# Leaving the state update out of the last chunk of a chunked linear attention

## The chip, the cores and the metric

The kernel runs on one core of a Trainium2 chip. The metric is the device time of one execution in microseconds (us). Before the change three runs gave 1142.96, 1143.62 and 1143.84 us, a median of 1143.62 us.

## The reference

The reference has three parts, one after the other, all in 32-bit floats. The first is a gated linear attention over 768 positions, for 4 batches, 8 heads and a head width of 48, with a complex decay `a` per position and channel:

```
mag = sqrt(a_re^2 + a_im^2);  a = a * min(mag, 0.999) / (mag + 1e-6)
for t in range(768):
    S = a[t] * S + k[t] (outer) v[t]        # S complex, k and v real
    y[t] = q[t] . Re(S)
```

Its output, seen as 3072 tokens of width 384, goes through `relu(x @ w_in)^2 @ w_out` (inner width 2048) and then through `(silu(x @ w_gate) * (x @ w_val)) @ w_out` (inner width 1536). The state S is not an output: only y of each position is.

## The kernel before

**Chunks.** The 768 positions are cut into six chunks of 128. Within a chunk the attention is written with matrices: with running products P of the decay, the keys are divided by P (tile `ks`) and the queries multiplied by it (tile `qs`); the masked product of the two, times v, is what the chunk's own positions give, and `qs` times the state that the chunk before left is the rest. The state that a chunk hands on is (its old state + scaled keys times v), scaled by the decay of the whole chunk.

**elem** (lines 493 to 649) makes these factors for one chunk. It computes the decay products, the chunk's total decay (`last`, `lm`), from that the scale `yB` (lines 596 to 601 and 632) and the new `phase` (line 630), and per group of two heads the tiles `qs` and `ks`. The keys are needed by position for the state, so `ks` is written to DRAM (`scr`, line 646) and read back in another layout as `kn` (line 647).

**mat** (lines 652 to 736) does the matrix part for one group of two heads; a chunk has four groups, called groups 0 to 3 here. TensorE transposes `ks` and `qs` into PSUM (`pt`), ScalarE copies them out (`kT`, `qT`). Lines 680 to 687 bring the scale of the state into the state's layout: a copy `ysrc` on ScalarE, two small products `pr`, a reciprocal `rho` on VectorE. Then come the scores `sc`, the masking `pb` on VectorE, the output `py` (from state and from scores), and its copy `ys`, which DMAs put into `xf`, the input of the next part (lines 713 to 725). Lines 726 to 735 are the state's update: eight products `pu` of `kn` and `vt`, and on VectorE two operations of 96x384, one that adds `pu` to the state and one that multiplies it by `rho`.

**moe1 and moe2** (lines 868 and 923) are the two other parts, chunk by chunk. Each float product is made of three products of 32-bit operands that are split into a high and a low half (`xh`, `xl`, `gh`, `gl`). One step of moe1 is nine matmuls into a tile `h`, ScalarE's relu, square and cast (`u`, `u`, `gh`), VectorE's `gl`, and two steps later nine matmuls into the accumulators `acc`. moe2 has two tiles per step, `pg` and `pv`, and a silu.

**prep2** (line 834) converts the 36 weight tiles of moe2: a load `wst`, three integer operations `wt` on VectorE, a cast into `wc` or `wr` on ScalarE, a subtraction on VectorE, and two operations on ScalarE that check `wst` (with their accumulators). A converted tile needs a free place. The first nine places are the attention's own tiles, when the last chunk has done with them (line 1040): `qs`, `ks`, `kn`, `cm`, `X` and four parts of `an`. The others are places of moe1's weights, as the last chunk of moe1 frees them.

**What sets the order.** `fast` (line 1024) pairs the attention of chunk n+1 with moe1 of chunk n; the last attention (chunk 5) goes beside moe1 of chunk 4, then moe1 of chunk 5 beside prep2, then moe2. All operations are recorded with a rank and a cost, and a list scheduler (`arrange`, line 172) puts them in the order in which each engine will issue them; it starts an operation as soon as its engine, its inputs and its buffers are free by its costs, the lowest rank first. Each engine then works through its list in that order. An edit in one place thus moves instructions around it.

Of the kernel before, what the change touches and what calls it, by code (L numbers as in the profile page):

```python
# [9 lines left out]
F32 = mybir.dt.float32  # L10
F32R = mybir.dt.float32r
I32 = mybir.dt.int32
AF = mybir.ActivationFunctionType
# [295 lines left out]
class Kern:  # L309
# [183 lines left out]
    def elem(self, n, g0, NG, res):  # L493

        nc, G, D, W = self.nc, self.G, self.D, self.W
        t0, nb = self.chunks[n]
        VW = NG * W
        gs = range(g0, g0 + NG)
        smn = lambda nm: self.e2.tile([128, nb, W], F32, name=nm, tag="smn", bufs=self.NSMN)
        sml = lambda nm: self.e2.tile([128, nb, W], F32, name=nm, tag="smk", bufs=self.NSMK)  # L500
        cs = lambda nm, shape: self.e2.tile(shape, F32, name=nm, tag=f"cs{len(shape)}", bufs=6 - len(shape))
# [3 lines left out]
        cols = lambda i, k=1: slice(i * W, (i + k) * W)  # L505
# [7 lines left out]
        def out(name, shape, i):  # L513
            if n:
                return self.e2.tile(shape, F32, name=name, tag=name, bufs=1)
            return self.slot(name, shape, F32, i)
# [5 lines left out]
        for i in gs:  # L522
# [17 lines left out]
            r = b0  # L540
# [19 lines left out]
        ks0 = slice(g0 * W // 32, g0 * W // 32 + K)  # L560
# [32 lines left out]
        sq2 = cs("sq2", [128, 2, K])  # L593
        nc.scalar.activation(out=sq2, in_=last, func=AF.Square)
        yield
        yB = self.e2.tile([128, VW], F32, name="yB", tag="yB", bufs=1)

        nc.vector.tensor_tensor(out=lm, in0=sq2[:, 0], in1=sq2[:, 1], op=ALU.add)
        nc.scalar.activation(out=sq2[:, 0], in_=lm, func=AF.Ln, bias=self.tiny[:, 1:2])
        yt = self.ytile[:, ks0]  # L600
        nc.scalar.activation(out=yt[:, :, 0], in_=sq2[:, 0], func=AF.Exp, scale=-0.5)
        for i in gs:
            if i % 2 == 0:

                for r in range(2):
                    self.cmul(an[:, :, r, cols(i, 2)], an[:, :, r, cols(i, 2)], an[:, :, 3, cols(i, 2)], 2 * W)
                    yield
                self.cmul(an[:, :, 2, cols(i, 2)], an[:, :, 1, cols(i, 2)], an[:, :, 2, cols(i, 2)], 2 * W)
                yield
                for c in range(2):  # L610
                    nc.vector.transpose(out=an[:, c, 3, cols(i, 2)], in_=X0[:, 32 * K * c + (i - g0) * W + 1:][:, 0:2 * W])
                yield
            pp = an[:, :, :, cols(i)]
            kq = keys.pop(i, None) or self.load(n, i, (self.k, self.q))
            kt, qt = kq[:, 0], kq[:, 1]
            psq = self.e2.tile([128, 2, nb, W], F32, name="Bt", tag="pp", bufs=self.NPP)
            nc.scalar.activation(out=psq, in_=pp, func=AF.Square)

            qs = out("qs", [128, nb, G, 2, D], 12 + i)
            for c in range(2):  # L620
                nc.vector.tensor_tensor(out=qs[:, :, :, c], in0=v4(pp[:, c]), in1=perm(qt), op=ALU.mult)
            yield
            pm = xy = sml("pm")
            nc.vector.tensor_tensor(out=pm, in0=psq[:, 0], in1=psq[:, 1], op=ALU.add)
            lp = sml("lp")
            nc.scalar.activation(out=lp, in_=pm, func=AF.Ln, bias=self.tiny[:, 1:2])
            iv = lp
            nc.scalar.activation(out=iv, in_=lp, func=AF.Exp, scale=-1.0)
            if i == g0:
                nc.vector.tensor_tensor(out=self.phase[:, :, ks0], in0=last,  # L630
                                        in1=yt[:, :, 0].unsqueeze(1).to_broadcast([128, 2, K]), op=ALU.mult)
                nc.vector.transpose(out=yB, in_=yt.rearrange("p k i -> p (k i)"))
            yield
            nc.vector.tensor_tensor(out=xy, in0=pm, in1=iv, op=ALU.mult)
            niv = xy
            nc.vector.scalar_tensor_tensor(out=niv, in0=xy, scalar=2.0, in1=iv, op0=ALU.subtract, op1=ALU.mult)
            yield
            ki = xy
            nc.vector.tensor_tensor(out=v4(ki), in0=perm(kt), in1=v4(niv), op=ALU.mult)
            ks = out("ks", [128, nb, G, 2, D], 16 + 2 * i)  # L640
            for c in range(2):
                nc.vector.tensor_tensor(out=ks[:, :, :, c], in0=v4(pp[:, c]), in1=v4(ki), op=ALU.mult)
            L = 32 * nb
            scr = self.dr.tile([self.B, L, G * 2 * D], F32, name="scr", tag="scr")
            kn = out("kn", [L, self.B, G, 2 * D], 17 + 2 * i)
            nc.sync.dma_start(out=scr.rearrange("b (j r) x -> (b j) (r x)", r=nb), in_=ks.rearrange("p r h c d -> p (r h c d)"))
            nc.sync.dma_start(out=kn.rearrange("p b h x -> p b (h x)"), in_=scr.rearrange("b t x -> t b x"))
            res[i] = dict(qs=qs, ks=ks, kn=kn, yB=yB[:, cols(i - g0)], vt=self.load_v(n, i))
            yield


    def mat(self, n, g, r, xf):
# [18 lines left out]
        for h in range(G):  # L671
            for src, dst, nm in ((ks, kT, "kT"), (qs, qT, "qT")):
# [4 lines left out]
                                        src[:, rr, h].rearrange("p c d -> p (c d)"), self.ident)  # L677
                nc.scalar.copy(dst[h], pt)
                yield
        rho = self.e2.tile([2 * D, G, B], F32, name="rho", tag="rho", bufs=self.N_rho)  # L680
        pr = bank("pr", [2 * D, G, B])
        ysrc = self.e2.tile([128, G, 2, D], F32, name="ysrc", tag="ysrc", bufs=self.N_ysrc)
        nc.scalar.copy(ysrc, yB.rearrange("p (h d) -> p h d", h=G).unsqueeze(2).to_broadcast([128, G, 2, D]))
        for h in range(G):
            nc.tensor.matmul(pr[:, h], ysrc[:, h].rearrange("p c d -> p (c d)"),
                             self.ident.rearrange("p (b j) -> p b j", b=B)[:, :, 0], start=True, stop=True)
        nc.vector.reciprocal(out=rho, in_=pr)
        yield
        pbs = []
        for h in range(G):  # L690
            sc = bank("sc", [L, B, L])
            for b in range(B):
                nc.tensor.matmul(sc[:, b], kT[h][:, L * b:L * b + L], qT[h][:, L * b:L * b + L], start=True, stop=True)
            pb = self.e2.tile([L, B, L], F32, name="pb", tag="pb", bufs=self.N_pb)
            nc.vector.tensor_tensor(
                out=pb, in0=sc,
                in1=self.mask[0:L, 0:L].unsqueeze(1).to_broadcast([L, B, L]), op=ALU.mult)
            pbs.append(pb)
            yield

            if h % 2 == 1:
                py = bank("py", [128, B, L])
                for b in range(B):
                    if n:
                        for hh in (h - 1, h):
                            o = 64 * (hh % 2)
                            nc.tensor.matmul(py[o:o + D, b], self.state[:, h0 + hh, b],
                                             qT[hh][:, L * b:L * b + L], start=True, stop=False)
                    for hh in (h - 1, h):
                        o = 64 * (hh % 2)  # L710
                        nc.tensor.matmul(py[o:o + D, b], vt[:, b, hh], pbs[hh][:, b], start=n == 0, stop=True)
                yield
                ys = self.e2.tile([128, B, L], F32, name="ys", tag="ys", bufs=self.N_ys)
                for hh in range(2):
                    o = 64 * hh
                    nc.scalar.activation(out=ys[o:o + D], in_=py[o:o + D], func=AF.Copy, scale=-1.0,
                                         accum_out=self.yflag[o:o + D, (n * self.H + h0 + h) // 2:][:, 0:1])
                    hd = (h0 + h - 1 + hh) * D
                    d0 = 0
                    while d0 < D:  # L720
                        row = hd + d0
                        m = min(D - d0, 128 - row % 128)
                        nc.sync.dma_start(out=xf[row % 128:row % 128 + m, row // 128],
                                          in_=ys[o + d0:o + d0 + m].rearrange("p b l -> p (b l)"))
                        d0 += m
                pu = bank("pu", [2 * D, 2, B, D])
                hs = h - 1
                for hh in range(2):
                    for b in range(B):
                        nc.tensor.matmul(pu[:, hh, b], kn[:, b, hs + hh], vt[:, b, hs + hh], start=True, stop=True)  # L730
                st = self.state[:, h0 + hs:h0 + hs + 2]
                if n:
                    nc.vector.tensor_tensor(out=st, in0=pu, in1=st, op=ALU.add)
                nc.vector.tensor_tensor(out=st, in0=st if n else pu,
                                        in1=rho[:, hs:hs + 2].unsqueeze(3).to_broadcast([2 * D, 2, B, D]), op=ALU.mult)
                yield
# [475 lines left out]
```

## Time and profile before

| | |
|---|---|
| median of three runs | 1143.62 us |
| the profiled execution | 1144.72 us, of which the span of instructions is 1142.6 us |
| TensorE (PE) busy | 1067.2 us, 93% of the span |
| VectorE (DVE) busy | 705.8 us, 62% |
| ScalarE (ACT) busy | 619.3 us, 54% |

A view of the profile gives starts in us from the beginning of the span. "PEld" is the load of a matmul's stationary operand. Nearly every line of the trace reads L306, the line that issues what was recorded, so groups are told apart by tile names. The attention of the last chunk runs its matrix part from 540 to 601 us, moe1 of chunk 5 begins at 614 us and moe2 at 685 us.

### The profile page before, as it was taken

The numbers are of one execution on the slowest core, as the hardware profiler recorded it, in microseconds if no ns is written. First come the engines' busy times: TensorE is split into PE (matmuls) and PEld (weight loads), VectorE is DVE, ScalarE is ACT, GpSimd is POOL, SyncE is SP. The second block draws the span as 40 slices with busy tenths as digits, with TensorE's granted clock in tenths as the row PEclk, the third lists the DMA queues.
The fourth block names the chain that finished last, engine by engine and source line by source line (L and its number), as shares of the span: only waits on it lengthen the run. The fifth ranks groups of instructions, "written<-read, shape, count | busy, mean of one in ns | idle before, by whom it ended". The sixth has DMA issues, their size and how long they took to land.

```text
span 1142.6 us, 16426 instructions
## 1 busy us (share of the span) xinstructions
PE 1067.2 (93%) x5890; PEld 899.9 (79%) x5890; DVE 705.8 (62%) x1485; ACT 619.3 (54%) x1334; POOL 1.0 (0%) x7
## 2 busy tenths in 40 slices
PE   2458979999999999999999999999999999999997
PEld 0346857888888888888887878888888888888886
DVE  6998999799789789789658883232232222322221
ACT  6479879957766766866669993131221222211221
POOL 0000000000000000000000000000000000000000
PEclk9968989999999999999999999999999999999998
DMA  5345355403612621522536441010010100000000
GB/s 141 125 128 160 111 150 164 131 15 92 160 55 71 164 72 56 154 56 69 153 99 211 148 124 56 1 56 1 1 56 1 56 1 1 28 1 1 28 1 31
DMA packets 102490, 89.25 MB, mean 78 GB/s; under 512 B 35072, under 2 KB 90368, under 8 KB 102400
## 3 DMA queue, kind: packets, MB, share of 16 engines
q1 hardware_dynamic: 102080, 87.93, 26.6%
q8 instruction: 48, 0.79, 0.3%
q14 instruction: 42, 0.34, 0.1%
q10 hardware_dynamic: 320, 0.20, 0.1%
HBM read 64.49 MB, written 18.87 MB: 73 GB/s over the span
## 4 chain that ended last, share of the span: by engine, by line
PE 79%; ACT 9%; DVE 6%; DMA 2%; SPq 2%; issue 1%; ACTq 0%; DVEq 0%
PE acc L306 26%; PE h L306 13%; PE pg L306 13%; PE pv L306 13%; PE py L306 4%; ACT wst L306 3%; PE pt L306 3%; PE sc L306 3%; PE pu L306 3%; SPq L306 2%; ACT u L306 2%; DVE an L306 1%; DMA wst<-in_moe_w_in_dram 1%; DVE AB L306 1%; ACT gh L306 1%
## 5 line engine op out<-in xcount | busy, mean ns | idle before, releaser
L306 ACT CAST gh<-u 128x512 fp32r<-128x512 f32 x168 | 104.2, 621 | 247.3 <-PE acc L306 217.0
L306 PE MATMUL h<-xh,wc 128*128 128x512 f32 x576 | 199.2, 400 | 3.2 <-ACT xh L306 2.4
L306 PE MATMUL acc<-gh,wr 128*128 128x512 f32 x576 | 195.7, 396 | 0.1
L306 DVE TENSOR_TENSOR gl<-u,gh 128x512 fp32r<-128x512 f32 x168 | 115.3, 688 | 126.6 <-ACT gh L306 125.9
L306 DVE TENSOR_TENSOR u<-pv,u 128x512 f32<-128x512 f32 x72 | 49.8, 692 | 204.6 <-PE pv L306 203.4
L306 PE MATMUL acc<-wr,gh 128*128 128x384 f32 x576 | 146.8, 335 | 0.0
L306 PE MATMUL pg<-xh,wc 128*128 128x512 f32 x396 | 134.8, 394 | 1.1 <-ACT xh L306 1.1
L306 PE MATMUL pv<-xh,wc 128*128 128x512 f32 x396 | 133.8, 392 | 1.3 <-ACT u L306 1.3
L306 PEld LDWEIGHTS h<-xh,wc 128*128 128x128 f32 x576 | 108.8, 190 | 27.7 <-ACT xh L306 2.7
L306 PEld LDWEIGHTS acc<-gh,wr 128*128 128x128 f32 x576 | 108.0, 188 | 23.3 <-issue 1.7
L306 PE MATMUL h<-xl,wc 128*128 128x512 f32 x288 | 114.4, 397 | 0.7 <-DVE xl L306 0.7
L306 PE MATMUL acc<-gl,wr 128*128 128x512 f32 x288 | 113.7, 395 | 0.2 <-DVE gl L306 0.2
L306 PEld LDWEIGHTS acc<-wr,gh 128*128 128x128 f32 x576 | 105.1, 188 | 5.2
L306 ACT ACTIVATE u<-pg 128x512 f32<-128x512 f32 x72 | 43.1, 599 | 104.7 <-PE pg L306 104.7
L306 PE MATMUL acc<-wr,gl 128*128 128x384 f32 x288 | 96.6, 335 | 0.0
L306 PEld LDWEIGHTS pv<-xh,wc 128*128 128x128 f32 x396 | 74.3, 188 | 18.3 <-ACT u L306 1.7
L306 PEld LDWEIGHTS pg<-xh,wc 128*128 128x128 f32 x396 | 74.3, 188 | 16.2 <-ACT xh L306 1.5
L306 ACT ACTIVATE u<-h 128x512 f32<-128x512 f32 x96 | 57.1, 597 | 46.1 <-PE h L306 41.0
L306 PE MATMUL pg<-xl,wc 128*128 128x512 f32 x198 | 78.2, 395 | 0.1
L306 PE MATMUL pv<-xl,wc 128*128 128x512 f32 x198 | 77.8, 393 | 0.0
L306 DVE SCALAR_TENSOR_TENSOR wt<-wst,wt 128x384 int32<-128x384 int32 x136 | 74.0, 551 | 1.7
L306 DVE TENSOR_TENSOR AB<-an 128x768 f32<-128x768 f32 x72 | 68.3, 948 | 0.6
(132 smaller groups left out, 1751.3 us busy)
## 6 DMA issues: line engine op xcount, KB each, us to landing
wst<-in_moe_w_out_dram SPq DMA_DIRECT2D x28, 384.0 KB, 3.5
scr<-ks SPq DMA_DIRECT2D x24, 384.0 KB, 2.5
kn<-scr SPq DMA_DIRECT2D x24, 384.0 KB, 3.5
wst<-in_moe_w_in_dram SPq DMA_DIRECT2D x16, 384.0 KB, 3.6
in<-in_k_dram SPq DMA_DIRECT2D x96, 48.0 KB, 2.0
in<-in_q_dram SPq DMA_DIRECT2D x96, 48.0 KB, 2.0
vt<-in_v_dram SPq DMA_DIRECT2D x48, 96.0 KB, 2.9
x2d<-x SPq DMA_DIRECT2D x18, 256.0 KB, 2.1
```

What stands on the lines that cost most here:

```text
L306: o.call(*o.args, **o.kw)
```

## The change

For the last chunk (`final`) elem no longer makes `yB` and the new `phase`, writes no `scr` and reads no `kn`; mat no longer makes `ysrc`, `pr` and `rho`, and leaves out `pu` and the two operations on the state. The output of the last chunk is computed as before. The tile of the tag `kn`, the third of the nine places of prep2, is then last used by chunk 4.

```diff
+        final = n == len(self.chunks) - 1
...
-        yB = self.e2.tile([128, VW], F32, name="yB", tag="yB", bufs=1)
-
         nc.vector.tensor_tensor(out=lm, in0=sq2[:, 0], in1=sq2[:, 1], op=ALU.add)
-        nc.scalar.activation(out=sq2[:, 0], in_=lm, func=AF.Ln, bias=self.tiny[:, 1:2])
-        yt = self.ytile[:, ks0]
-        nc.scalar.activation(out=yt[:, :, 0], in_=sq2[:, 0], func=AF.Exp, scale=-0.5)
+        if not final:
+            yB = self.e2.tile([128, VW], F32, name="yB", tag="yB", bufs=1)
+            nc.scalar.activation(out=sq2[:, 0], in_=lm, func=AF.Ln, bias=self.tiny[:, 1:2])
+            yt = self.ytile[:, ks0]
+            nc.scalar.activation(out=yt[:, :, 0], in_=sq2[:, 0], func=AF.Exp, scale=-0.5)
...
-            if i == g0:
+            if i == g0 and not final:
...
+            kn = None
+            if not final:
+                scr = self.dr.tile([self.B, L, G * 2 * D], F32, name="scr", tag="scr")
+                kn = out("kn", [L, self.B, G, 2 * D], 17 + 2 * i)
+                nc.sync.dma_start(out=scr.rearrange("b (j r) x -> (b j) (r x)", r=nb), in_=ks.rearrange("p r h c d -> p (r h c d)"))
+                nc.sync.dma_start(out=kn.rearrange("p b h x -> p b (h x)"), in_=scr.rearrange("b t x -> t b x"))
+            res[i] = dict(qs=qs, ks=ks, kn=kn, yB=None if final else yB[:, cols(i - g0)], vt=self.load_v(n, i))
...
+        if kn is not None:
+            rho = self.e2.tile([2 * D, G, B], F32, name="rho", tag="rho", bufs=self.N_rho)
...
+            nc.vector.reciprocal(out=rho, in_=pr)
+            yield
...
+                if kn is None:
+                    yield
+                    continue
                 pu = bank("pu", [2 * D, 2, B, D])
```

The scheduler's order moves with it. In the rows below a number behind a tile's name only tells tiles of one name apart.

TensorE, the last group of the last attention, before (`h_1534` is a step of moe1 of chunk 4, `acc_1335` an accumulator of the same):

```order
L306 MATMUL pt<-ident,qs 96x128 x4
L306 MATMUL pr<-ident,ysrc 96x4 x2
L306 MATMUL sc<-qT,kT 128x128 x4
L306 MATMUL h_1534<-xh,wc 128x512
...
L306 MATMUL sc<-qT,kT 128x128 x4
L306 MATMUL py<-qT,state 48x128 x2
L306 MATMUL py<-pb,vt 48x128
L306 MATMUL pu<-vt,kn 96x48 x4
L306 MATMUL py<-pb,vt 48x128
...
L306 MATMUL pu<-vt,kn 96x48 x4
L306 MATMUL acc_1335<-gh,wr 128x512
```

and now (`h_1514` is the next step of moe1):

```order
L306 MATMUL pt<-ident,qs 96x128 x4
L306 MATMUL sc<-qT,kT 128x128 x4
L306 MATMUL acc_1335<-gh,wr 128x512
L306 MATMUL acc_1335<-gl,wr 128x512
L306 MATMUL sc<-qT,kT 128x128 x4
...
L306 MATMUL py<-qT,state 48x128 x2
L306 MATMUL py<-pb,vt 48x128 x2
...
L306 MATMUL h_1514<-xh,wc 128x512
```

The `pr` and `pu` are gone, the two score products stand two matmuls apart instead of nine, and three steps of moe1 of chunk 4 follow the last `py` instead of two.

ScalarE, where moe1 of chunk 4 ends, before (`xh<-xf` splits the input of moe1 of chunk 5, `xh<-x_1648` that of moe2's first chunk, and `h_1547` is the last step of moe1 of chunk 4):

```order
L306 ACTIVATE u<-h_1547 128x512
L306 ACTIVATE wst,flg_60<-wst,wlow_98 128x384
L306 ACTIVATE u<-u 128x512
L306 CAST xh<-xf 128x512
L306 CAST gh<-u 128x512
L306 CAST xh<-xf 128x512 x2
...
L306 COPY x_1554<-acc_1337 128x512
...
L306 CAST wc<-wt 128x384
L306 CAST xh<-x_1648 128x512 x2
```

and now (`h_1522` is that last step, `x_1623` moe2's first input):

```order
L306 CAST xh<-xf 128x512 x2
L306 ACTIVATE u<-h_1522 128x512
L306 CAST xh<-xf 128x512
L306 ACTIVATE u<-u 128x512
...
L306 CAST gh<-u 128x512
...
L306 COPY x_1529<-acc_1337 128x512
L306 CAST xh<-x_1623 128x512 x2
```

The split of `xf` has moved ahead of the last step's relu, and the split of moe2's input follows the copies at once.

TensorE, where moe1 of chunk 5 ends and moe2 begins, before (`acc_1587` is moe1's last accumulator):

```order
L306 MATMUL acc_1587<-gh,wr 128x512
L306 MATMUL pv<-xh,wc 128x512 x2
...
L306 MATMUL pv<-xh,wc 128x512
L306 MATMUL pg<-xl,wc 128x512
...
L306 MATMUL pg<-xh,wc 128x512
L306 MATMUL pv<-xh,wc 128x512
L306 MATMUL pv<-xl,wc 128x512
```

and now (`acc_1562` is that accumulator):

```order
L306 MATMUL acc_1562<-gh,wr 128x512
L306 MATMUL pv<-xh,wc 128x512
L306 MATMUL pg<-xh,wc 128x512
L306 MATMUL pg<-xl,wc 128x512
...
L306 MATMUL pg<-xh,wc 128x512
L306 MATMUL pv<-xh,wc 128x512
L306 MATMUL pv<-xl,wc 128x512
```

Before, fifteen matmuls (seven `pv`, eight `pg`) stood between the last `acc` and moe2's second `pv`; now ten do (one and nine), since more of the first pair has moved ahead of moe1's steps.

## Rows read from the trace of the kernel before

**Rows 1.** The page, part 1: busy us, share of the span, instructions

```profile
PE 1067.2 (93%) x5890; PEld 899.9 (79%) x5890; DVE 705.8 (62%) x1485; ACT 619.3 (54%) x1334; POOL 1.0 (0%) x7
```

**Rows 2.** Stretch, length, busy us (instructions) of PE, PEld, DVE, ACT, POOL; PEclk; DMA

```profile
540.00:560.00 20.00, 20.00 (x144) 17.07 (x143) 14.55 (x31) 14.89 (x30) 0.00 (x0) 1.00 0.44 135
560.00:580.00 20.00, 20.00 (x149) 17.08 (x148) 10.34 (x23) 10.89 (x24) 0.00 (x0) 1.00 0.52 144
...
610.00:620.00 10.00, 8.87 (x39) 6.68 (x38) 7.25 (x15) 9.52 (x26) 0.00 (x0) 1.00 0.68 218
...
640.00:660.00 20.00, 20.00 (x90) 16.55 (x89) 18.43 (x38) 20.00 (x55) 0.00 (x0) 1.00 0.53 159
...
680.00:700.00 20.00, 18.38 (x81) 14.51 (x80) 10.25 (x19) 13.19 (x29) 0.00 (x0) 1.00 0.24 79
```

**Rows 3.** The chain that ended last, 545 to 565 us: start, us, what

```profile
545.72 0.26 PE pr L306 x4
...
549.08 2.04 PE h L306 x9
...
558.24 1.32 PE pu L306 x16
559.55 0.88 PE pt L306 x8
...
563.65 2.19 PE h L306 x9
```

**Rows 4.** A group over all six chunks: count, busy us, mean ns, idle before

```profile
L306 ACT COPY ysrc<-yB 128x192 f32<-128x192 f32 x24 | 8.4, 350 | 4.7 <-DVE yB L306 4.7
```

**Rows 5.** TensorE's instructions from 607 to 627 us: start, us, what, idle before

```profile
607.84 0.39 PE L306 MATMUL h<-xh,wc 128*128 128x512 f32 x1
...
614.51 0.39 PE L306 MATMUL h<-xh,wc 128*128 128x512 f32 x1
...
618.37 0.39 PE L306 MATMUL h<-xh,wc 128*128 128x512 f32 x1
619.88 0.50 PE L306 MATMUL pg<-xh,wc 128*128 128x512 f32 x1 [1.12 <-ACT xh L306]
...
627.30 0.40 PE L306 MATMUL h<-xh,wc 128*128 128x512 f32 x1
```

**Rows 6.** The way of moe2's first input; last, landing times around there

```profile
613.96 0.34 SPq L306 DMA_DIRECT2D x<-x2d  x1
...
619.21 1.13 ACT L306 CAST xh<-x 128x512 fp32r<-128x512 f32 x2
...
DMA to landing us min/median/max: 4.8/4.9/6.6
```

**Rows 7.** ScalarE and TensorE where moe2 begins

```profile
685.08 1.11 ACT L306 COPY x<-acc 128x512 f32<-128x512 f32 x2
686.04 0.71 ACT L306 ACTIVATE wst<-wst,wlow 128x384 f32<-128x384 f32 x1
...
688.37 1.28 ACT L306 ACT_TABLE_LOAD   x1
689.66 0.60 ACT L306 ACTIVATE u<-pg 128x512 f32<-128x512 f32 x1
...
688.62 0.40 PE L306 MATMUL pg<-xh,wc 128*128 128x512 f32 x1
690.31 0.50 PE L306 MATMUL pv<-xh,wc 128*128 128x512 f32 x1 [1.30 <-ACT u L306]
```

**Rows 8.** ScalarE's first conversion of prep2; the DMA queue's issues around it

```profile
590.66 0.52 ACT L306 CAST wc<-wt 128x384 fp32r<-128x384 f32 x1
...
558.31 0.38 SPq L306 DMA_DIRECT2D wst<-in_moe_w_out_dram  x1
...
586.40 1.79 SPq L306 DMA_DIRECT2D xf<-ys  x3
597.70 0.37 SPq L306 DMA_DIRECT2D wst<-in_moe_w_val_dram  x1
```

More of the change, by code (lines that the diff above doesn't have):

```diff
@@ L643, in elem @@
             L = 32 * nb
[L644 to L648, printed above, removed]
+            kn = None
[5 more added lines that the diff above has]
+            res[i] = dict(qs=qs, ks=ks, kn=kn, yB=None if final else yB[:, cols(i - g0)], vt=self.load_v(n, i))
             yield
@@ L679, in mat @@
                 yield
[L680 to L688, printed above, removed]
+        if kn is not None:
+            rho = self.e2.tile([2 * D, G, B], F32, name="rho", tag="rho", bufs=self.N_rho)
+            pr = bank("pr", [2 * D, G, B])
+            ysrc = self.e2.tile([128, G, 2, D], F32, name="ysrc", tag="ysrc", bufs=self.N_ysrc)
+            nc.scalar.copy(ysrc, yB.rearrange("p (h d) -> p h d", h=G).unsqueeze(2).to_broadcast([128, G, 2, D]))
+            for h in range(G):
+                nc.tensor.matmul(pr[:, h], ysrc[:, h].rearrange("p c d -> p (c d)"),
+                                 self.ident.rearrange("p (b j) -> p b j", b=B)[:, :, 0], start=True, stop=True)
+            nc.vector.reciprocal(out=rho, in_=pr)
+            yield
         pbs = []
```

## The prediction, made before the result was known

> **What bounds the kernel now.** I read the busy times first. TensorE is busy for 93% of the span, VectorE for 62, ScalarE for 54 [rows 1]. A busy share is an average, so I took the stages that the change touches. From 540 to 580 us, the matrix part of the last attention beside moe1 of chunk 4, TensorE is busy without a gap at a granted clock of 1.00 (the 2.4 GHz level), VectorE for 14.55 and then 10.34 of 20 us, ScalarE for 14.89 and then 10.89 of 20 [rows 2]. The reader is to see that the other engines have room there and TensorE has none. Next comes the chain that ended last: through that stretch it runs from one TensorE group to the next, and `pr` and `pu` stand in it [rows 3]. So what these take there is on the path.
>
> Two later places matter, since TensorE gets there sooner after the change. At 610 to 620 and at 680 to 700 us it is not full: 8.87 of 10 and 18.38 of 20 [rows 2]. The instructions name the waits: at 618.6 us for ScalarE's `xh` [rows 5], at 688.9 us for ScalarE's silu, which follows its table load [rows 7]. And from 640 to 660 us ScalarE is busy for 20.00 of 20 us beside TensorE's 20.00 [rows 2]: there two engines are near the limit together, which makes the main doubt below.
>
> **The change part by part.** *The products.* In the chain the sixteen matmul instructions of a group's `pu` (eight products, each in two passes) take 1.32 us, and the four of `pr` 0.26 us [rows 3]. The chunk has four groups: 4 x 1.32 = 5.28 us and 4 x 0.26 = 1.04 us, together 6.32 us. I take all of it as gain, because TensorE neither waits nor idles in that stretch: what stands behind these products is moe1, which is ready. The bound from below is that the last group's share, 1.58 us, is lost in waits for `kT`, `qT` or `pb`, since the scores now stand closer together; that leaves 4.7.
>
> *The turns between kinds of matmul.* Nine matmuls of moe1 take 2.04 us behind scores and 2.19 us behind `pr` [rows 3]: a turn costs up to 0.15 us. The new order has 32 turns where there were 36, counted from the steps before the last attention's matrix part to moe2. Two of the four are entries into moe1's matmuls, 2 x 0.15 = 0.3 us of gain; the range is 0 to 0.6.
>
> *ScalarE, VectorE and the DMA queue.* Four copies `ysrc` of 350 ns [rows 4] leave ScalarE, eight operations on the state and four reciprocals leave VectorE, and eight DMAs leave the queue. Beside a full TensorE I price all that at nothing; if the cover were gone, ScalarE's 4 x 0.35 = 1.4 us would be the gain. No wait is added.
>
> *What the freed place does.* The first conversion of prep2 starts at 590.66 us [rows 8], when the attention's last transposes let go of its tiles; the weights behind it then share the few buffers of `wt`. Now the third weight finds `kn` free, and in ScalarE's new list its cast stands ahead of the last group's copies `kT` and `qT`. So conversions start earlier, in a stretch where ScalarE had 9.1 of 20 us to spare [rows 2]. That is why I expect it to keep pace with a TensorE that is 6.6 us further on.
>
> *The gap at 619 us.* From the first step of moe1 of chunk 5 at 614.51 to its fourth at 627.30 us TensorE issues 48 matmuls (three steps of nine `h`, and 21 of `pg`, `pv` and `acc`) [rows 5]. At 2.04/9 = 0.227 us each they need 10.88 us; 12.79 passed, so 1.9 us are lost. The cause is a row of steps: moe2's input is loaded into the buffer of `xf`, so the load waits for the split of `xf`; it was issued at 613.96 us, and its own split began at 619.21 [rows 6]. The load lands 4.8 to 6.6 us after its issue [rows 6]. In the new order the split of `xf` stands ahead of the last relu of moe1 of chunk 4, and the attention ends one step of moe1 earlier. The last `h` of that step was issued by 607.84 + 0.23 = 608.07 us [rows 5], so the old load came 5.9 us behind it. With two casts ahead of the relu, only the relu, one cast and its subtraction on VectorE are left: two ScalarE operations in a row take 1.13 us [rows 6], and with as much again for the subtraction and the hand-overs I get some 2.7 us. The load then lands 7.5 to 9.3 us behind that step. TensorE has 27 + 18 matmuls to issue before it needs it, 45 x 0.227 = 10.2 us, and the first two casts of its split take 1.13 us [rows 6], the subtraction some 0.7. So most of the gap goes: I take 1.6 us of gain, with bounds 0 and 1.9.
>
> *The gap at 689 us.* TensorE's last `pg` of 688.62 us ends its issue at 688.85 and the next `pv` starts at 690.31 [rows 7]: 1.46 us, because all three PSUM buffers wait for silu, which waits for ScalarE's copies of the accumulators (from 685.08), two splits and a table load of 1.28 us. The new order has ten matmuls in front of that wait where there were fifteen, so TensorE comes to it 5 x 0.227 = 1.1 us earlier; ScalarE's list has one check of `wst` less between the copies and the table load, some 0.6 us by its row of 0.71 [rows 7]. I take 1.1 - 0.6 = 0.5 us of loss, with bounds from 1.4 of gain (ScalarE gets there with nothing left to do) to 2.0 of loss (it is as late as before and the cover is gone).
>
> *The sum.* 6.32 + 0.3 + 1.6 - 0.5 = 7.7 us. The profiled execution took 1144.72 us, its span 1142.6; less 7.7 that is 1137.0. The three runs have a median of 1143.62, 1.1 us below the profiled one, so I predict 1135.9 us. The bounds together: at best 6.32 + 0.6 + 1.9 + 1.4 = 10.2 us, at worst 4.7 + 0 + 0 - 2.0 = 2.7 us.
>
> *A rule to weigh.* The price of `pu` stands on its spacing, 1.32 / 16 = 82 ns, though it moves only 48 columns; a transpose `pt`, with 128 columns, has 0.88 / 8 = 110 ns [rows 3]. The Trainium skill, "TensorE: Matmul & The Clock Gate", section "Back-to-back issue gap", puts a matmul of 1 to 64 columns at about 25 ns. By that rule the sixteen would be worth 0.4 us and a group's `pr` 0.1, and the first term 2.0 us instead of 6.32. Its section on LDWEIGHTS gives columns / 1.2, 80 ns for 96 columns, an estimate that the 82 ns agree with: the load of `kn` is what the removed products pay for. I go by the row.
>
> **The rivals.** *ScalarE holds the gain back (in part or whole).* From 640 us on ScalarE is as full as TensorE [rows 2]. If its conversions do not start earlier, moe1 of chunk 5 soon waits for its relu and casts, and the end moves only by what ScalarE itself is spared: 1.4 us of `ysrc`. In full that gives 1143.6 - 1.4 = 1142.2 us; halfway, 1139.0. For it speaks the 20.00 of 20; against it that ScalarE has idle time before 600 us, and that the slots of prep2 are freed by moe1's own progress, so its work is paced by TensorE.
>
> *The products are cheaper than their spacing.* If only the columns counted, sixteen `pu` would take 16 x 48/128 x 0.110 = 0.66 us, `pr` next to nothing, and the first term were 2.7 us: 1143.6 - (2.7 + 0.3 + 1.6 - 0.5) = 1139.5 us. Against it: in the chain the transposes start when the last `pu` is done, and 1.32 us are seen to pass [rows 3]. This is the side on which the page's 25 ns stand.
>
> *Slower: a cast blocks ScalarE's line.* ScalarE works in order. The third weight's cast now stands ahead of the last group's `kT`; that weight's load stands in the DMA queue behind `ys` of an earlier group. The queue has paused for long in this stretch: between the end of one issue at 588.2 and the next at 597.70 us lie 9.5 us [rows 8]. If such a pause falls on this load, ScalarE stands at the cast, TensorE has no transposed keys, and with moe1's step ahead used up it waits up to 9.5 us in the last group, and what leans on `xf` waits too. The change is slower than before from a wait of 7.7 us on; with 9.5 us and the gap at 619 us kept (1.6) it comes to 1143.6 - 7.7 + 9.5 + 1.6 = 1147.0 us. Against it: it is the third of prep2's loads, which in the old trace was issued at 558.31 us, 32 us before the first cast [rows 8].
>
> *Nothing is gained.* If moe1 of chunk 5 begins when `xf` lands and not when TensorE is done, the time stays at 1143.6. Against it: the new order has one step of moe1 more between the last `py` and the end of moe1 of chunk 4, 18 x 0.227 = 4.1 us in which `xf` can land.
>
> **How the numbers follow.** The forecast, all terms about as above (1134.3 to 1138.0 us): 0.68. ScalarE holds back: 0.15, of which 0.12 still ends below 1141.3. Cheaper products: 0.03. More than forecast, below 1134.3, because the gap at 689 us closes as well: 0.06. Nothing gained: 0.03. Slower: 0.05. A difference of 0.2% (2.3 us) is about what a measurement of this kernel can tell from no change. Faster by more than that: 0.68 + 0.12 + 0.03 + 0.06 = 0.89; within it 0.03 + 0.03 = 0.06; slower 0.05. The range of 8 in 10 leaves out the slow cases and the fullest form of the first rival, and has room for the best case of the bounds: 1133.8 to 1140.3 us.
>
> **What would show it.** In the changed profile the chain through the last attention must still be TensorE's, without `pu` and `pr`, and moe1 of chunk 5 must begin some 6.6 us earlier, near 608 us; `xh` must no longer stop `pg`; the gap before moe2's second `pv` must be about 2 us; the first cast of prep2 must come ahead of 585 us. I am wrong if TensorE idles in the last group behind ScalarE's `kT` or `qT`, if moe1 of chunk 5 runs at more than 2.04 us per nine matmuls, or if its first step starts earlier by much less than the removed time.

## The result and the profile after

| | before | after |
|---|---|---|
| median | 1143.73 us (4 runs, 1142.96 to 1144.24) | 1133.31 us (4 runs, 1132.51 to 1133.58) |
| ratio, 95% interval | | 0.9906 [0.9893, 0.9918] |
| profiled execution, its span | 1144.72, 1142.6 us | 1133.17, 1131.1 us |

The change is worth 10.4 us here, and 12.0 in a second set (below). The forecast was 7.7 us, and the time lies 0.5 us below its range.

The page's busy times, which answer to [rows 1], lose 11.6 us on TensorE, 4.3 on VectorE and 2.1 on ScalarE:

```profile
PE 1055.6 (93%) x5810; PEld 891.0 (79%) x5810; DVE 701.5 (62%) x1471; ACT 617.2 (55%) x1328; POOL 0.9 (0%) x7
```

The windows that answer to [rows 2] (start and end, length, then the busy time of PE, PEld, DVE, ACT and POOL, the granted clock, DMA share and GB/s):

```profile
540.00:560.00 20.00, 20.00 (x135) 16.94 (x133) 14.35 (x30) 14.87 (x30) 0.00 (x0) 1.00 0.32 88
560.00:580.00 20.00, 20.00 (x165) 17.15 (x163) 11.29 (x22) 13.57 (x31) 0.00 (x0) 1.00 0.37 106
640.00:660.00 20.00, 20.00 (x90) 16.54 (x89) 18.47 (x39) 20.00 (x57) 0.00 (x0) 1.00 0.53 156
660.00:680.00 20.00, 17.79 (x76) 13.79 (x74) 14.67 (x30) 19.90 (x50) 0.00 (x0) 1.00 0.28 90
```

TensorE is as full as before in the last attention. From 660 to 680 us, where moe1 now gives way to moe2, it has holes (17.79 of 20), as it had from 680 to 700 us before [rows 2], while ScalarE is busy for 19.90. The chain through two groups of the last attention (start, duration, engine and tile), which answers to [rows 3]:

```profile
560.36 0.89 PE sc L306 x8
561.25 0.24 PE h L306
561.49 0.89 PE sc L306 x8
562.38 1.84 PE h L306 x8
564.23 1.90 PE py L306 x32
566.12 0.57 PE pt L306 x4
...
572.16 1.79 PE sc L306 x16
573.95 0.57 PE py L306 x6
574.51 0.89 PE acc L306 x3
575.41 1.67 PE py L306 x26
```

It is still all TensorE, without `pr` and `pu`. Look also at `py`: in the first of these groups its 32 instructions stand in one row. In the same view of the kernel before, the group that follows [rows 3] has its `py` cut twice by a single matmul of moe1:

```profile
567.63 0.36 PE py L306 x4
567.98 0.43 PE acc L306
568.41 0.35 PE py L306 x2
568.76 0.42 PE acc L306
569.19 1.67 PE py L306 x26
```

The last attention has five such rows of `py` now, where it had eight. That is the first thing the prediction did not see.

The prediction read the chain up to 565 us. Further on, the same view of the kernel before leaves TensorE at 588 us:

```profile
585.89 2.17 PE h L306 x9
588.07 0.02 issue
588.09 0.60 ACT u L306
```

From there it runs mostly through ScalarE, up to moe2's second `pv` at 690 us. In the changed kernel it stays with TensorE up to 601 us, and from 616 to 680 us it is mostly ScalarE's. ScalarE thus had little to spare before the change as well. The gain passes here with ScalarE's work starting earlier too (its first cast of prep2 below); no run holds that work alone back.

TensorE's instructions that answer to [rows 5] and [rows 7] (an idle time before one, and what ended it, in brackets), and ScalarE's that answer to [rows 6] and [rows 8]:

```profile
605.42 0.39 PE L306 MATMUL h<-xh,wc 128*128 128x512 f32 x1
609.29 0.39 PE L306 MATMUL h<-xh,wc 128*128 128x512 f32 x1
609.52 0.40 PE L306 MATMUL pg<-xh,wc 128*128 128x512 f32 x1
...
672.44 0.39 PE L306 MATMUL acc<-gh,wr 128*128 128x512 f32 x1
673.50 0.50 PE L306 MATMUL acc<-gh,wr 128*128 128x512 f32 x1 [0.67 <-ACT gh L306]
674.22 0.50 PE L306 MATMUL acc<-gl,wr 128*128 128x512 f32 x1 [0.22 <-DVE gl L306]
...
678.28 0.40 PE L306 MATMUL pg<-xh,wc 128*128 128x512 f32 x1
680.04 0.50 PE L306 MATMUL pv<-xh,wc 128*128 128x512 f32 x1 [1.36 <-ACT u L306]
```

```profile
574.28 0.51 ACT L306 CAST wr<-wt 128x384 fp32r<-128x384 f32 x1 [0.82 <-DVE wt L306]
...
606.11 1.15 ACT L306 CAST xh<-x 128x512 fp32r<-128x512 f32 x2
```

moe1 of chunk 5 begins at 605.42, not 614.51 us. Its first `pg` follows `h` with no wait: `xh` is cast 3.4 us ahead of it. The first cast of prep2 comes at 574.28, not 590.66 us. The wait for silu is 0.06 us longer than before. The waits for `gh` and `gl` ahead of it stood there before the change too, 0.57 us shorter:

```profile
682.18 0.98 PE L306 MATMUL acc<-gh,wr 128*128 128x512 f32 x2
683.38 0.50 PE L306 MATMUL acc<-gl,wr 128*128 128x512 f32 x1 [0.22 <-DVE gl L306]
```

Last, what lies behind TensorE's last product `tot`, which starts at 1134.27 us before and at 1123.99 after. The view is that of the program's last line, ten waits of SyncE with their first and last start; first the kernel before, then after:

```profile
L1207 SPq EVENT_SEMAPHORE  x10: 17/28/28, 1140.0 to 1142.6; - x10
```

```profile
L1215 SPq EVENT_SEMAPHORE  x10: 17/28/28, 1129.8 to 1131.0; - x10
```

The same ten waits took 2.6 us and take 1.2. In the kernel before, SyncE pauses 1.29 us among them; afterwards it does not.

**The account.** The cost of a TensorE instruction is counted here as the distance from its start to the next start, summed by tile. The anchors are the first `pt` of chunk 4 (449.92 us before, 448.71 after), the first `h` of moe1 of chunk 5, the second `pv` of moe2, and `tot`.

| stretch | before | after | gain | of which |
|---|---|---|---|---|
| start to chunk 4's first `pt` | 449.92 | 448.71 | 1.21 | differs between executions (below) |
| to moe1 of chunk 5 | 164.59 | 156.71 | 7.88 | `pu` 5.66, `pr` 1.13, `py` 0.89, `sc` 0.37, the rest -0.17 |
| to moe2's second `pv` | 75.80 | 74.61 | 1.19 | gap at 619 us 1.80, waits for `gh`, `gl` and silu -0.64, the rest 0.03 |
| to `tot` | 443.96 | 443.95 | 0.0 | |
| to the end of the span | 8.35 | 7.07 | 1.28 | SyncE's pause |

Without the first line this is 10.35 us, and the medians differ by 10.42. In all the traces of this study the first `pt` of chunk 4 lies between 448.1 and 451.5 us, so the first line is not counted as the change's.

### The profile page after: what moved, and what is told of

It reads as the page before. It is cut to its first block, busy times and chain, and to the rows that moved or that the text cites. A ratio compares the mean times of both kernels' runs of the same rounds, so it can differ in the third digit from the quotient of the medians.

```text
span 1131.1 us, 16229 instructions
## 1 busy us (share of the span) xinstructions
PE 1055.6 (93%) x5810; PEld 891.0 (79%) x5810; DVE 701.5 (62%) x1471; ACT 617.2 (55%) x1328; POOL 0.9 (0%) x7
## 4 chain that ended last, share of the span: by engine, by line
PE 78%; ACT 9%; DVE 7%; DMA 2%; SPq 2%; issue 2%; ACTq 0%; DVEq 0%
PE acc L306 25%; PE pg L306 13%; PE pv L306 13%; PE h L306 13%; PE py L306 4%; PE pt L306 3%; PE sc L306 3%; ACT wst L306 3%; PE pu L306 2%; SPq L306 2%; DVE AB L306 2%; ACT u L306 1%; DVE an L306 1%; ACT gh L306 1%; DVE wt L306 1%
```

## The experiments

The kernel before ran along in each set: median 1144.41 us beside the first four, 1144.33 beside the next four, 1144.76 beside the last three. Ratios are to that.

**The scale alone put back** into the changed kernel (`yB`, `ysrc`, `pr`, `rho`).

```diff
-        if kn is not None:
+        if True:
```

> The changed kernel, with the scale of the last chunk put back alone: yB, ysrc, pr, rho, without pu and without the state. By the count of TensorE's starts in the two traces pr is worth 1.13 us, and since the order cuts the py of a group as often as before (8 rows of py instead of 5) 3 cuts at some 0.33 us come on top: the last attention takes 2.1 us longer than in the changed kernel, the gap at 619 us stays closed, the time is about 1135.4 us. By the forecast's sizes (1.04 for pr, 0.3 for turns) 1.3 us, 1134.6 us.

Measured: 1138.42 us, 0.9952 [0.9939, 0.9966]. From chunk 4's first `pt` to moe1 of chunk 5 it takes 159.88 us, 3.17 more than the changed kernel: `pr` 1.14, `py` 1.08 (eight rows again; 0.26 of it lies in chunk 4, where nothing was edited), `sc` 0.37, `acc` 0.51. So `pr` costs some two and a half times its own time, because with it the order tears `py` as before. The other way round, `pu` and the state alone are worth 164.59 - 159.88 = 4.71 us, less than their own 5.66. The gap at 619 us stays closed. The whole loss, 5.1 us between the medians, is larger than the 2.1 expected: in the profiled execution one fall of the clock (last section) cost another 1.56 us.

**The place of `kn` held**: round trip put back, and one column of `kn` read at each group's end, no products.

```diff
-            kn = None
-            if not final:
...
+            res[i] = dict(qs=qs, ks=ks, kn=None if final else kn, held=kn,
...
+                    nc.vector.tensor_copy(self.ytile[:, 0, 1:2], r["held"][:, 0, 0, 0:1])
```

> The changed kernel, with the key round trip (scr, kn) of the last chunk put back, and a read of one column of kn at the end of each group, so that kn's place is free for prep2 as late as before; no products. If the freed place closed the gap at 619 us (the split of xf stands behind the last relu again), the gap comes back with up to 1.8 us; if the gap closed because the attention ends earlier, it stays closed. The attention stage itself as in the changed kernel (within 0.2 us). SyncE's list is as long as before: if its length makes the pause of 1.3 us among its last waits, that comes back too: 1136.4 us with both, 1133.3 with neither.

Measured: 1135.48 us, 0.9919 [0.9905, 0.9932]; the pause of SyncE is back (8.31 us behind `tot`). The gap is back too:

```profile
609.90 0.39 PE L306 MATMUL h<-xh,wc 128*128 128x512 f32 x1
611.41 0.50 PE L306 MATMUL pg<-xh,wc 128*128 128x512 f32 x1 [1.12 <-ACT xh L306]
```

So the freed place did close the gap, by way of ScalarE's order: here the split of `xf` stands behind the last relu of moe1 of chunk 4 again. But the waits at 673 and 680 us shrink by 1.3 us in return, the stretch to moe1 of chunk 5 takes 0.47 us less (I had allowed 0.2), and from chunk 4's first `pt` to `tot` this kernel takes 675.25 us, the changed one 675.27. The freed place is worth nothing in the end. Nor do the conversions need it to start earlier: with the place held, the first cast of prep2 comes at 581.81 us, still 8.9 us ahead of the kernel before.

**`py` held together, in the last chunk of the kernel before.** The scheduler lets `py` start only when both masks are done, puts it ahead of all else, and `pu` behind it.

```diff
+                if n == len(self.chunks) - 1:
+                    for o in nc.ops[k0:k1]:
+                        o.after.update(masked)
+                        o.rank -= 10 ** 6
```

> The kernel before, all its work, but in the last chunk the scheduler holds the py of a group together (4 rows of py instead of 8, pu behind the last py). By the count a cut costs some 0.33 us: 1.3 us less in the last attention, whose products are all there. The split of xf now stands ahead of the last relu, so the gap at 619 us closes as well if the order makes it: together 3.1 us, 1140.6 us; without the gap 1142.4. If a turn costs 0.15 us as the forecast had it and most turns stay, 0.6 us or nothing.

Measured: 1142.27 us, 0.9976 [0.9967, 0.9985]. With four rows of `py` instead of eight, and all products in place, `py` costs 1.30 us less from chunk 4 on (1.17 of it in the last chunk), `sc` 0.52, `pu` 0.41: 2.23 us. The other tiles take 0.24 more, so the stretch is 1.99 us shorter, 0.50 for each row that goes. That is more than I expected. By the forecast's count nothing should have been gained: between moe1's matmuls and the attention's there are 42 turns in this order where there were 36. The gap near 619 us did not close, it broke up into smaller waits (1.75 us together). There my expectation rested on a misreading: in this order too the split of `xf` stands behind the last relu of moe1, as in the kernel before. So this run does not speak against the cause.

**The state update of chunk 4 left out as well.**

```diff
+        nostate = n >= len(self.chunks) - 2
...
-            if not final:
+            if not nostate:
```

> The changed kernel, with the state update of chunk 4 left out as well (its output for the last chunk then lacks what chunk 4 hands on). By the count chunk 4's attention gets shorter by pr 1.13, pu 5.65 and 3 cuts of py of some 0.33, 7.8 us, with no gap of prep2 in it: 1125.5 us. By the forecast's sizes 6.6 us, 1126.7 us. If much of the last chunk's gain came from the places it frees and not from TensorE's time, less than 5 us.

Measured: 1127.74 us, 0.9856 [0.9842, 0.9869]. From chunk 4's first `pt` to moe1 of chunk 5: 149.86 us, 6.85 less than the changed kernel. My 7.8 was wrong in one point: chunk 4 keeps its eight rows of `py`. The products' 6.78 us are left, and they are TensorE's own time. The medians differ by 5.6 us only, since 0.78 us is lost again behind `tot`, where SyncE pauses at another point (last section).

**`py` held together in chunks 1 to 5** of the changed kernel (the edit above for all `n` but 0).

> The changed kernel, with the py of a group held together by the scheduler in chunks 1 to 5 (4 rows of py in a chunk instead of 10, 11, 11, 8 and 5). If each cut costs what the run with uncut py in the last chunk showed (2.23 us for 4 rows, over py, sc and pu), the 25 rows that go are worth 9 to 12 us, less what the wait for both masks costs: 1122 to 1126 us. If cuts are cheap (0.15 us a turn) some 4 us, 1129 us. If py now waits for VectorE's masks, nothing or a loss.

Measured: 1129.21 us, 0.9872 [0.9854, 0.9890]: some 4 us below the changed kernel, not 9 to 12. That is the size that I had put beside cheap cuts. Yet `py` costs 7.6 us in each chunk where it took up to 9.5, 7.1 us less over the five chunks. So the rows are not cheap, but what they cost in the last chunk cannot be multiplied by their number. In chunks 4 and 5 only 0.3 us is left of it: their stretch is 6.4 us shorter, but 27 matmuls of moe1 (6.1 us at 0.227) now stand ahead of it. Part is lost again: in chunk 4 the transposes `pt`, with waits in them, take 8.35 us instead of 6.67, and the waits for `gh`, `gl` and silu, at 668 and 673 us there, grow by 0.8 us.

**ScalarE's second check left out** for moe2's weights.

```diff
+            if self.used[2] <= 2 * self.F1 // 128:
                 nc.scalar.activation(out=hi, in_=hi, func=AF.Relu, scale=-1.0, bias=self.wlow2, accum_out=f2)
```

> The changed kernel without the second of ScalarE's two checks on each weight of moe2 (36 operations of some 0.7 us, 25 us of ScalarE between 575 and 750 us; that part of the check of the inputs is left out). If ScalarE is what TensorE waits for at 673 and 680 us (3.1 us in the changed kernel), most of the wait at 673 us and part of that at 680 us go: 1.5 to 3 us less, 1130.3 to 1131.8 us. If these waits come from the chain acc, copies, table load, silu alone, under 0.5 us.

Measured: 1129.29 us, 0.9866 [0.9851, 0.9882]. The stretch from moe1 of chunk 5 to moe2's second `pv` takes 71.89 us instead of 74.61, and no wait is left at either place. ScalarE's backlog, with the checks in it, made both, also the one that I had put down to the copies, the table load and silu. The median is 4.0 us below the changed kernel, more than my 1.5 to 3: 2.7 us come from this stretch, 0.6 from the one ahead of it, and the rest is not explained.

**SyncE's list made as long as before**: eight small loads in the last chunk's elem of the changed kernel.

```diff
+            for j in range(8):
+                nc.sync.dma_start(out=self.ytile[0:32, 0, 1 + j:2 + j], in_=self.v[0, 0, 0:32, j:j + 1])
```

> The changed kernel with eight small loads (32 numbers each, read by nobody) in SyncE's list during the last chunk's elem, so that the list is as long again as before the change. If its length sets the pause of 1.3 us among SyncE's last waits, the span after TensorE's last product is 8.3 us again instead of 7.1 and the time 1134.6 us, with TensorE as in the changed kernel. If the pause comes from anything else the change left out, 1133.3 us.

Measured: 1135.66 us, 0.9922 [0.9908, 0.9936]. TensorE's stretches are those of the changed kernel (156.57, 74.60 and 443.94 us, `tot` at 1124.73), and the pause is back. The time is 1.1 us above the 1134.6 that I gave; in the profiled execution chunk 4 is reached 0.9 us later.

```profile
L1218 SPq EVENT_SEMAPHORE  x10: 17/28/28, 1130.5 to 1132.9; - x10
```

**`pu` with half of `kn` as its stationary operand**, in the last chunk of the kernel before.

```diff
+                        half = D if n == len(self.chunks) - 1 else 2 * D
-                        nc.tensor.matmul(pu[:, hh, b], kn[:, b, hs + hh], vt[:, b, hs + hh], start=True, stop=True)
+                        nc.tensor.matmul(pu[0:half, hh, b], kn[:, b, hs + hh, 0:half], vt[:, b, hs + hh], start=True, stop=True)
```

> The kernel before, but in the last chunk pu takes 48 of kn's 96 columns as its stationary operand (half of the state, which nobody reads after that chunk); as many products, as many columns moved. If the load of the stationary operand sets the 82 to 88 ns, the 64 products cost about half: 2.8 us less in the last attention, 1141 us. If a product of 48 columns has a floor of its own, its 88 ns stay and the time is that of the kernel before.

Measured: 1140.99 us, 0.9967 [0.9955, 0.9979]. The instructions of `pu` in the last attention (nanoseconds, smallest, median and largest; first and last start; the stationary operand's size), in the kernel before and here:

```profile
L306 PEld LDWEIGHTS pu<-vt,kn x64: 159/165/165, 557.8 to 599.7; 128*96 128x96 f32 x64
L306 PE MATMUL pu<-vt,kn x64: 205/248/283, 558.1 to 599.7; 128*96 128x48 f32 x64
```

```profile
L306 PEld LDWEIGHTS pu<-vt,kn x64: 119/125/125, 559.6 to 597.3; 128*48 128x48 f32 x64
L306 PE MATMUL pu<-vt,kn x64: 204/208/243, 559.6 to 597.3; 128*48 128x48 f32 x64
```

As many products of as many columns, but from start to start they take 3.16 us instead of 5.65, 49 ns each instead of 88: the load sets the pace. (The edit also halves the rows that a product writes, and the run does not separate the two. But the load's own record shrinks by 40 ns and the spacing by 39.) The median falls by 3.3 us and not by 2.5, because the order moved here too: one cast of the split of `xf` stands ahead of the last relu, and the stretch with the gap at 619 us is 1.40 us shorter. The Trainium skill, "TensorE: Matmul & The Clock Gate", section on LDWEIGHTS, makes a load proportional to its columns, and the trace agrees; the 25 ns that its section "Back-to-back issue gap" gives for an isolated matmul of 1 to 64 columns are not reached here even with half the load.

**The changed kernel once more.**

> The changed kernel once more, unedited. By the account TensorE's last product comes 9.1 us earlier after the first products of chunk 4 than in the kernel before, and SyncE's pause is absent (span after the last product 7.1 us); what lies ahead of chunk 4 moves by about 1 us from execution to execution, as the granted clock falls at other moments between 50 and 160 us. So the difference of the medians is 10.3 us here too. If the clock of the start was part of the gain, it is nearer 9 or 12.

Measured: 1132.72 us, 0.9894 [0.9879, 0.9909]. The difference of the medians is 12.0 us, not 10.3, although the stretches repeat: 156.75, 74.55, 443.94 and 6.92 us. From chunk 4's first `pt` to the end, this execution is 10.5 us ahead of the trace of the kernel before, the first one 10.35. The other 1.5 us lie ahead of that `pt` or in the spread of the medians (the kernel before is 1 us higher in this set than in the first). No trace of the kernel before stands in this set, so that stays open, and the change is worth 10 to 12 us.

**The second check on VectorE**, as a minimum.

```diff
+                nc.vector.tensor_reduce(out=self.small[:, self.nsmall:self.nsmall + 1], in_=hi, axis=mybir.AxisListType.X, op=ALU.min)
```

> The changed kernel, with ScalarE's second check of moe2's weights (relu of a bound less the square, summed) made a minimum of the squares on VectorE, compared with the bound at the end. If ScalarE alone makes the waits at 673 and 680 us, they are gone as in the run without that check: 3.2 us less than the changed kernel, 1130 us. If VectorE becomes late with gl or the integer operations (36 operations of some 0.45 us more, at 14.7 of 20 us busy), waits of acc for gl come in their place and at most 1.5 us is left.

Measured: 1131.17 us, 0.9878 [0.9862, 0.9895], 1.6 us below the changed kernel beside it, which is near the 1.5 of the second alternative. On TensorE the gain is larger, 71.60 instead of 74.55 us up to moe2's second `pv`; this execution reached chunk 4 0.9 us later. VectorE keeps up at 19.07 of 20 us busy, and no wait takes the place of those that go:

```profile
660.00:680.00 20.00, 20.00 (x89) 16.31 (x88) 19.07 (x42) 17.10 (x38) 0.00 (x0) 1.00 0.44 137
```

**Both, the check on VectorE and `py` held together.**

> The changed kernel with both: the check on VectorE, and the py of chunks 1 to 5 held together. The two act in different places, so the gains add: 3.2 and 5.0 us, about 1125 us. If the checks' time on VectorE meets the masks of the last chunk, the last attention gets longer and it is 1127 us or more.

Measured: 1125.12 us, 0.9833 [0.9817, 0.9850]: 7.6 us below the changed kernel of the same set and 19.6 below the kernel before. It leaves nothing out.

## Why the prediction was wrong in its size

The direction and the main mechanism were right: 7.88 of 10.35 us are TensorE's time in the last attention, and most of what ScalarE holds back it held back before as well. Two terms of the sum failed, the turns by 0.79 us and what stands behind the last product by 1.28; had either come as forecast, the time would lie inside the range.

**The turns between kinds of matmul** were priced by a wrong rule. I put them at 0.3 us, with 0.6 as the upper bound; `py`, `sc` and the rest gave 0.89 + 0.37 - 0.17 = 1.09. I had priced a turn by what a step of moe1 pays behind it, 0.15 us, and counted the turns between moe1 and the attention, 36 and 32; a `py` that is cut by `pu` is not among them. The traces show that turns are not alike. A row of `py` is dear: the `sc` in front of it takes 0.205 us to the next start instead of 0.112, its last instruction 0.20 instead of 0.10, the matmul of moe1 behind it 0.34 instead of 0.23, and a cut leaves pairs of `py` unpaired that otherwise start within 0.01 us of each other. A turn from `pt` or `sc` to moe1 costs next to nothing: their last one takes 0.03 instead of 0.11 us, the matmul of moe1 behind it 0.32. What counted was rows of `py`, eight before and five after, and they stood in the trace. Putting `pr` back brought all eight rows back, and uniting four rows in the kernel before gave 1.99 us, although the turns rose from 36 to 42.

**"ScalarE, VectorE and the DMA queue: nothing"** failed by more, 1.28 us, and not where I looked. The eight DMAs that leave cost nothing in the stage. But SyncE's list is shorter, and with that a pause at the end of the program is gone. I read no row behind the last matmul. The run with eight idle loads brought the pause back.

**The products** were right in kind and a little small: 6.79 us where I had 6.32. The chain gives an instruction a duration, and the start-to-start distance in a row of `pu` is 0.085 us, not 0.082. The bound from below, waits in the last group, did not occur. That the load of `kn` is what the removed products pay for is borne out by the run with half of it.

**The gap at 619 us** gave 1.80 us where I took 1.6, and its cause was right: with the place held, the gap came back. **The gap at 689 us** was a loss of 0.64 with the wait for `gh` ahead of it, where I took 0.5. But I treated the two as independent. The run with the place held shows that they are one: ScalarE, with its checks of the weights, is late by a certain time, and most of what TensorE no longer waits for at 619 it waits for at 673 and 680. As a sum the two terms (+1.1 forecast, +1.19 measured) came out right, in part by luck: the loss that I forecast at the second gap arose at the wait for `gh`. My account of the second gap, copies and table load, was incomplete, since leaving out one check closed it.

**The rivals.** "ScalarE holds the gain back" had a true core, 3 us that TensorE waits at 673 to 680 us, but before the change it waited there for most of that already. Against that rival I had the idle time of ScalarE and the order of prep2; that the chain itself ran through ScalarE from 588 us I had not read. "Products cheaper", "a cast blocks ScalarE" and "nothing" did not occur. "More than forecast" did, though not for the reason that I gave: that gap did not close. The range ended 2 us below the forecast. I wrote that it has room for the best case of the bounds, but those 10.2 us give 1133.4 us, 0.4 below its end at 1133.8. And that best case was summed from bounds of the terms that I had: one I had bounded too narrowly, and one I did not have.

Of the five signs, three came as said: no `pu` or `pr` in the chain, `xh` no longer stops `pg`, the first cast ahead of 585 us. The gap before moe2's second `pv` is 1.5 us (678.51 to 680.04) and not 2, because part of the wait now stands ahead of it at `gh`. moe1 of chunk 5 began 9.1 us earlier instead of 6.6, of which 1.2 are the start of the program.

## What to carry to other kernels

Price a removed kind of matmul from start to start, its neighbours included: see which rows of other products it was cutting, and what one such cut costs on either side. Read the chain to its end, since it can change engines behind the stretch that you edit. A wait that closes ahead of an engine near its limit can be given back at that engine's next deadline, as here, so sum such gaps as one term. And read the rows behind the last product, since a list that gets shorter can change what happens there.

## What had not been expected of the hardware

**A pause at a fixed place of SyncE's list.** In the five traces whose SyncE list has 919 or 920 recorded instructions, SyncE pauses 1.14 to 1.30 us right behind the 913th, among waits that are otherwise 0.07 us apart. In the seven lists of 901 to 912 there is no such pause. (The run with two chunks left out, 900 instructions, pauses for 0.98 us behind another instruction, in the closing steps; that one is not explained.) The Trainium skill, "Runtime: NRT & Kernel Launch", section "Instruction fetch mechanics", says that lists are fetched in blocks of 256 instructions and that a jump out of the fetched part stalls. The fixed place and the jump over the unused path just before it fit that, and the section's "mostly hidden" does not fit the 1.2 us. No row here names a fetch, and each of the five programs with the pause also issues eight DMAs more than the changed kernel, so the cause stays open.

**A fall of the clock after a wait.** With the scale put back, TensorE waited 2 us for silu, as in other runs, but this time the granted clock dropped:

```profile
680.83 0.40 PE L306 MATMUL pg<-xh,wc 128*128 128x512 f32 x1
683.07 0.51 PE L306 MATMUL pv<-xh,wc 128*128 128x512 f32 x1 [1.84 <-ACT u L306]
```

```profile
684.00:688.00 4.00, 4.00 (x13) 3.10 (x12) 1.38 (x2) 0.99 (x2) 0.00 (x0) 0.57 0.83 277
688.00:692.00 4.00, 4.00 (x22) 3.61 (x21) 0.69 (x1) 1.11 (x2) 0.00 (x0) 1.00 0.00 0
```

A mean of 0.57 from 684 to 688 us means that most of it ran at the lower level, 1.2 GHz: 13 matmuls are counted there, and 22 in the next 4 us at 1.00. It cost 1.56 us (445.51 from moe2's second `pv` to `tot` instead of 443.95). With `py` held together in all chunks, a wait of nearly the same length (2.0 us of idle issue at 673 us) brought no such fall. What tips it no run here shows.
